# Attention into a gated unit on one Trainium2 core: gated loads, one causal select per chunk, and paired half-row transposes, with a new instruction order

## The chip, the cores and the metric

The kernel runs on one core of a Trainium2 chip. The metric is device time in microseconds (us). The engines go by the names that the profile gives them: PE is TensorE (PEld its weight loads), DVE is VectorE, ACT is ScalarE, POOL is GpSimd, and SP issues the DMA transfers. Each run has a state, fast or slow; only fast runs are compared, and it is said where that was not possible.

## The reference, cut to what matters

```python
# q, k, v: (8 batches, 8 heads, 576, 64); s: (8, 8, 576)
scores = q @ k.T / 8
cum    = cumsum(maximum(s, 0))
scores = where(causal, -1e9, scores + minimum(cum_k - cum_q, 0))
x      = softmax(scores) @ v                     # then heads side by side: (8, 576, 512)
gate_pre = sum(conv_w[k] * shift(x, 4 - k) for k in range(5))
out    = (sigmoid(gate_pre) * (x @ w_val)) @ w_out
```

## The kernel before

The work is cut into 32 chunks: eight batches times four pairs of heads. Each step of a chunk is a task with an engine, an assumed duration and a priority. A small planner in the kernel simulates the engines with those durations and fixes, while the program is built, the order in which each engine gets its instructions. The chip then follows that order; only the waits are decided at run time. Priorities (`DUE`) and choices of engine (`CHOICE`) are tables of constants, found by a search against the planner's own clock.

```python
def qk_T(b, p):                       # TensorE: one pair of heads, 8 full transposes, one PSUM bank
    pt = slot["qt", b, p] = bank(("qt", b, p), 128, 1024, BF16)...
    for which in range(2):
        for j in range(4):
            nc.tensor.transpose(pt[:, which, j * 128:(j + 1) * 128],
                                qkbs[which][b % 2][:, j, p * 128:(p + 1) * 128], ident)

def mask(n, hh):                      # POOL: zero the future in the diagonal blocks, one head
    d = slot["Pt", n][:, hh, 0:512].rearrange("k (g q) -> k g q", g=4)
    nc.gpsimd.affine_select(out=d, in_=d, pattern=[[0, 4], [1, 128]], compare_op=ALU.is_ge,
                            fill=0.0, base=0, channel_multiplier=-1)

def tap(e, n, sh):                    # one tap of the causal convolution, on DVE or on POOL
    ...
    if e == "POOL":                   # two instructions
        nc.gpsimd.tensor_tensor(tmp[:, o:S], xs[...], r.to_broadcast(...), ALU.mult)
        nc.gpsimd.tensor_tensor(gp[:, o:S], tmp[:, o:S], gp[:, o:S] if o else xs[:, 2:], ALU.add)
    elif o:                           # one instruction
        nc.vector.scalar_tensor_tensor(gp[:, o:S], slot["x", n][...], r, gp[:, o:S], ALU.mult, ALU.add)
    ...

plan = Plan(dict(P=3, gp=2, th=6, ot=3, qkf=3))     # buffers per kind; ot: output tiles
...
add("POOL", 0.6, n + due("mask") + 0.01 * hh, lambda n=n, hh=hh: mask(n, hh), [t])   # for hh in 0, 1
...
t = add(("DVE", "POOL"), (0.73, 2.25), n + due("tap") + sh * due("dtap"), ..., pick=("tap", 4 * n + sh - 1))
...
plan.total = plan.run()
with tc.manual_schedule():
    for t in plan.order:
        t["emit"]()
```

Four taps a chunk make 128 taps; before, 18 of them run on POOL and 110 on DVE. ACT takes the exponentials (96 of 128x1024) and the tanh of the gate, DVE normalises, and POOL also casts Q and K and scales V by the decay weights `w`, which come from `s`.

## Time and profile before

| | before |
|---|---|
| time, median of 3 runs | 211.16 us (209.36 to 211.21) |
| span of the profiled run | 209.3 us |
| busiest engines | DVE 178.0, PE 175.4, ACT 163.1, POOL 161.9 us |
| chain that ended last | DVE 27%, ACT 24%, PE 23%, no POOL |
| mean granted clock of TensorE | 0.965 |

A busy time is a sum over one engine; the chain is the sequence of work that set the end, followed backwards through the waits. Four engines are busy for 77 to 85% of the span, so none is a bound alone. The lines themselves are in the prediction below.

### The profile page before, as it was taken

How to read it: one execution, taken by the hardware profiler on the slowest of the kernel's cores; microseconds unless marked ns; L12 is line 12 of the kernel's file. 1: busy time of each engine (PE TensorE's matmuls, PEld its weight loads, DVE VectorE, ACT ScalarE, POOL GpSimd, SP SyncE). 2: the span in 40 equal slices, each digit the busy share in tenths (PEclk: the TensorE clock that was granted, in tenths of full speed). 3: DMA queues.
4: the chain of work that ended last, by engine and by line, in shares of the span. 5: the costliest groups of instructions: out<-in, count | busy, mean ns of one | idle time of the engine just before them, and what ended most of it. 6: DMA issues, size and time to landing. Idle time of an engine off the chain costs nothing.

```text
span 209.3 us, 6007 instructions
## 1 busy us (share of the span) xinstructions
PE 175.4 (84%) x2392; PEld 119.4 (57%) x2411; DVE 178.0 (85%) x311; ACT 163.1 (78%) x205; POOL 161.9 (77%) x179
## 2 busy tenths in 40 slices
PE   1697885999969998689899799989899999979950
PEld 0455763475736766367665567565576556645620
DVE  3847969999888998669999999999999998999810
ACT  3279497778999899987996998799987998553330
POOL 4276486499959998999589999967975899999300
PEclk9999797599999999999999999999999999999995
DMA  4999999997999699999999821951149220222551
GB/s 147 238 279 288 361 147 216 354 271 207 244 281 323 138 319 221 323 297 226 222 383 307 190 107 25 184 147 49 54 110 219 81 77 1 99 104 75 180 180 61
DMA packets 69230, 40.48 MB, mean 193 GB/s; under 512 B 47109, under 2 KB 63493, under 8 KB 69194
## 3 DMA queue, kind: packets, MB, share of 16 engines
q1 hardware_dynamic: 69194, 40.01, 72.7%
q8 instruction: 21, 0.34, 0.7%
q14 instruction: 15, 0.12, 0.2%
HBM read 30.57 MB, written 9.44 MB: 191 GB/s over the span
## 4 chain that ended last, share of the span: by engine, by line
DVE 27%; ACT 24%; PE 23%; DMA 8%; issue 8%; SPq 7%; ACTq 0%; DVEq 0%
ACT P L592 13%; DVE gp L647 9%; PE banks L660 8%; DMA qkf<-in_moe_w_val_dram 6%; PE banks L672 6%; DVE xn L623 4%; PE banks L613 4%; ACT QKT L561 4%; ACT th L653 4%; DVE glu L666 3%; DVE gp L649 3%; PE banks L566 3%; SPq L515 3%; SPq L534 2%; ACT ot L677 2%
## 5 line engine op out<-in xcount | busy, mean ns | idle before, releaser
L592 ACT ACTIVATE P<-banks 128x1024 bf16<-128x1024 f32 x96 | 94.8, 1039 | 11.8 <-PE banks L566 9.9
L647 DVE SCALAR_TENSOR_TENSOR gp<-banks,ratio,gp 128x574 f32<-128x574 bf16 (+2 forms) x85 | 67.5, 804 | 2.4 <-POOL gp L645 1.7
L598 POOL TENSOR_SCALAR_AFFINE_SELECT P<-P 128x512 bf16<-128x512 bf16 x64 | 39.6, 640 | 11.3 <-ACT P L592 11.1
L566 PE MATMUL banks<-QKT 64*128 64x128 bf16 (+4 forms) x576 | 38.9, 249 | 8.8 <-ACT P L592 5.6
L660 PE MATMUL banks<-xT,wv 128*128 128x288 bf16 x256 | 41.7, 294 | 2.1 <-DVE glu L666 0.9
L672 PE MATMUL banks<-wo,glu 128*128 128x512 bf16 x141 | 38.3, 379 | 2.5 <-ACT QKT L561 0.8
L528 POOL TENSOR_TENSOR Vp<-vst,w 128x650 bf16<-128x650 f32 x29 | 37.6, 1316 | 1.3 <-DMA vst<-in_v_dram 1.3
L613 PE MATMUL banks<-Vp,P 128*128 128x65 bf16 x960 | 37.3, 198 | 1.3 <-ACT P L592 1.2
L613 PEld LDWEIGHTS <-P 128*128 128x128 bf16 x960 | 35.3, 101 | 5.4 <-issue 2.1
L566 PEld LDWEIGHTS <-QKT 64*128 64x128 bf16 x576 | 20.1, 97 | 27.0 <-issue 20.6
L653 ACT ACTIVATE th<-gp,halfw 128x576 f32<-128x576 f32 x32 | 25.2, 793 | 7.1 <-DVE gp L647 3.6
L660 PEld LDWEIGHTS <-wv 128*128 128x128 bf16 x256 | 22.8, 99 | 13.9 <-issue 6.1
L666 DVE SCALAR_TENSOR_TENSOR glu<-th,banks 128x288 bf16<-128x288 f32 x64 | 28.0, 445 | 1.1 <-PE banks L660 1.0
L623 DVE TENSOR_TENSOR xn<-banks,recs 128x640 bf16<-128x640 f32 x32 | 26.2, 818 | 0.3
L561 ACT COPY QKT<-banks 128x1024 bf16<-128x1024 bf16 x25 | 25.3, 1049 | 1.2 <-PE banks L557 1.1
L677 ACT COPY ot<-banks 128x512 f32<-128x512 f32 (+1 forms) x26 | 15.2, 587 | 11.4 <-PE banks L672 6.9
L672 PEld LDWEIGHTS <-glu 128*128 128x128 bf16 x160 | 14.6, 97 | 15.5 <-issue 2.7
L649 DVE SCALAR_TENSOR_TENSOR gp<-xT,ratio,banks 128x576 f32<-128x576 bf16 x25 | 20.1, 809 | 1.6 <-ACT xT L635 0.9
L644 POOL TENSOR_TENSOR tmp<-xT,ratio 128x576 f32<-128x576 bf16 (+3 forms) x18 | 20.6, 1142 | 1.0 <-ACT xT L635 0.5
L645 POOL TENSOR_TENSOR gp<-tmp,gp 128x573 f32<-128x573 f32 (+2 forms) x11 | 15.7, 1428 | 3.1 <-DVE gp L647 2.3
L631 PE MATMUL banks<-ident,xn 128*128 128x128 bf16 x160 | 14.2, 220 | 2.9 <-DVE xn L623 1.2
L518 POOL CAST qb<-qkf 128x2048 bf16<-128x2048 f32 x7 | 13.2, 1890 | 2.2 <-DMA qkf<-in_q_dram 2.2
(63 smaller groups left out, 169.2 us busy)
## 6 DMA issues: line engine op xcount, KB each, us to landing
out_dram<-ot SPq DMA_DIRECT2D x32, 256.0 KB, 2.9
qkf<-in_q_dram SPq DMA_DIRECT2D x7, 1024.0 KB, 8.5
qkf<-in_k_dram SPq DMA_DIRECT2D x7, 1024.0 KB, 9.9
vst<-in_v_dram SPq DMA_DIRECT2D x28, 256.0 KB, 5.4
vst<-in_v_dram SPq DMA_DIRECT2D x15, 128.0 KB, 4.0
first<-in_q_dram SPq DMA_DIRECT2D x4, 256.0 KB, 3.4
first<-in_k_dram SPq DMA_DIRECT2D x4, 256.0 KB, 3.4
tail<-in_q_dram SPq DMA_DIRECT2D x8, 128.0 KB, 8.7
```

The lines of the kernel that those rows point to most:

```text
L528: eng.tensor_tensor(Vps[b % 2][:, :, h], vst[:, :, h], w[:, :, b * 8 + 2 * p:b * 8 + 2 * p + 2].unsqueeze(3).to_broadcast([128, NKB, 2, 65 ...
L561: copy[e](QKTs[b % 2][:, :, p, 0:512].rearrange("d w (x j) -> d w x j", j=4), slot["qt", b, p].rearrange("d w (j x) -> d w x j", j=4))
L566: nc.tensor.matmul(ps[:, hh, c0:c0 + nq], QKTs[b % 2][r, 1, p, k0:k0 + 128], QKTs[b % 2][r, 0, p, q0:q0 + nq], **kw)
L592: nc.scalar.activation(out=slot["Pt", n][:, :, step * 512:(step + 1) * 512], in_=slot["s", n, step], func=AF.Exp, scale=0.125)
L598: nc.gpsimd.affine_select(out=d, in_=d, pattern=[[0, 4], [1, 128]], compare_op=ALU.is_ge, fill=0.0, base=0, channel_multiplier=-1)
L613: nc.tensor.matmul(ps[:, hh, qb * 65:qb * 65 + 65], lhsT, Vps[b % 2][:, kb, 2 * p + hh, :], start=(kb == 0), stop=(kb == qb))
L623: nc.vector.tensor_tensor(xns[b % 2][:, :, p * 128:(p + 1) * 128].rearrange("t g (h d) -> t h g d", h=2), pv[:, :, :, 0:64], recs[:, n].un ...
L647: nc.vector.scalar_tensor_tensor(gp[:, o:S], slot["x", n][:, 0:S - o], r, gp[:, o:S], ALU.mult, ALU.add)
L653: nc.scalar.activation(out=th, in_=slot["g", n], func=AF.Tanh, scale=halfw[:, n % 4, :])
L660: nc.tensor.matmul(ps, wv[:, dc, c * 128:(c + 1) * 128], xTs[b % 2][:, dc, 2 + o:290 + o], start=(dc == 0), stop=(dc == 3))
L666: nc.vector.scalar_tensor_tensor(glus[b % 2][:, c, o], slot["t", n][:, o], 1.0, slot["v", n, hf], ALU.add, ALU.mult)
L672: nc.tensor.matmul(ps, glus[b % 2][:, c, WIN[i]:WIN[i] + 128], wo[:, c, :], start=(c == 0), stop=(c == 3))
```

## The change

Its intent: save TensorE time with half-row transposes that run two at a time, save POOL time with one select for both heads, and keep early loads from piling up in the DMA queue. Output buffers grow from three to five, and all priorities and engine choices are searched anew.

```diff
-DUE = dict(w=-69.33, lwv=-4.26, ...)          # (cut: 71 priorities before, 90 after, all new)
+DUE = dict(w=-211.74, lwv=14.18, ..., lq0d=12.42, ...)
+BEHIND = 11.22
-              tap="0000000010...0000",        # 18 taps on POOL
+              tap="0000010010...0000",        # 28 taps on POOL
 ...
                 if e == "SP":
-                    idle_at[e] = now + 0.06
                     dma_free = max(dma_free, now + 1.2) + us
+                    idle_at[e] = max(now + 0.06, dma_free - BEHIND)     # the planner's gate
 ...
-    plan = Plan(dict(P=3, gp=2, th=6, ot=3, qkf=3))
+    plan = Plan(dict(P=3, gp=2, th=6, ot=5, qkf=3))
 ...
+    def qk_T2(b, m):                 # two pairs of heads, 32 half-row transposes, two PSUM banks
+        for w in range(2):
+            for p in range(2):
+                for j in range(4):
+                    for g in range(2):
+                        r = slice(64 * g, 64 * g + 64)
+                        nc.tensor.transpose(pt[:, g, w, p, j, :],
+                            qkbs[w][b % 2][r, j, (2 * m + p) * 128:(2 * m + p + 1) * 128], ident[r, r])
 ...
-    def mask(n, hh):
-        d = slot["Pt", n][:, hh, 0:512].rearrange("k (g q) -> k g q", g=4)
-        nc.gpsimd.affine_select(out=d, in_=d, pattern=[[0, 4], [1, 128]], ...
+    def mask(n):
+        d = slot["Pt", n][:, :, 0:512].rearrange("k h (g q) -> k h g q", g=4)
+        nc.gpsimd.affine_select(out=d, in_=d, pattern=[[0, 2], [0, 4], [1, 128]], ...
 ...
-                es += [t] if i else [add("POOL", 0.6, ..., mask(n, hh), [t]) for hh in range(2)]
+                es += [t] if i else [add("POOL", 0.75, n + due("mask"), lambda n=n: mask(n), [t])]
```

The tasks of the first batch (loads, casts, scalings) also get searched priorities instead of fixed ones, so the start may come in another order too.

## The prediction

> **What bounds the kernel now.** I read the page first for the engines' busy time, then the table by stretches, then the chain of waits, then the groups by line, and last the timeline of single engines for the spacing of instructions. First, busy time:
>
> ```profile
> PE 175.4 (84%) x2392; PEld 119.4 (57%) x2411; DVE 178.0 (85%) x311; ACT 163.1 (78%) x205; POOL 161.9 (77%) x179
> ```
>
> Four engines lie within 16 us of each other; no single one is the bound by itself. The table by stretches (length, then busy time of PE, PEld, DVE, ACT, POOL) shows where the other 31 us of DVE, the longest, went:
>
> ```profile
> 0.00:30.00 30.00, 20.21 (x277) 15.44 (x278) 19.13 (x35) 18.85 (x26) 17.17 (x34) 0.94 0.95 246
> 30.00:190.00 160.00, 143.52 (x2056) 97.65 (x2071) 150.33 (x261) 138.57 (x173) 139.32 (x142) 0.98 0.74 191
> 190.00:209.30 19.30, 11.68 (x66) 6.31 (x65) 8.52 (x17) 5.64 (x9) 5.46 (x5) 0.89 0.40 135
> ```
>
> In the middle 160 us DVE is 94% busy (150.3), PE 90%, ACT and POOL 87%. DVE idles about 11 us in the start, 10 in the middle and 11 in the end. So the middle is bound by DVE with PE and ACT close behind, and start and end are bound by latency. The chain that ended last agrees:
>
> ```profile
> DVE 27%; ACT 24%; PE 23%; DMA 8%; issue 8%; SPq 7%; ACTq 0%; DVEq 0%
> ```
>
> It passes through three engines in turn; GpSimd (POOL) is not on it at all, so POOL had slack before. Its end is a plain wait for a buffer: the last ACT copy of an output tile waits until a store has left one of the three output buffers.
>
> ```profile
> 199.24 0.59 ACT ot L677
> ...
> 199.84 3.50 DMA out_dram<-ot
> ...
> 203.44 0.59 ACT ot L677
> ```
>
> The timeline has the last output matmuls from 197.31 for 4.48 us, that is to 201.8, so this wait costs about 203.4 - 201.8 = 1.6 us.
>
> **What the Trainium skill says.** "TensorE: Matmul & The Clock Gate", Part 3 (Packing small matmuls): matmuls in different row groups run at the same time in one array, their starts a few ns apart. The trace agrees. Seven score matmuls of 64 columns, alternating between the halves, take 0.27 us, the last alone about 0.20: (0.27 - 0.20)/6 = 12 ns apart. Four full transposes of 128 columns take 0.39, one 0.22: (0.39 - 0.22)/3 = 57 ns apart.
>
> ```profile
> 60.62 0.27 PE L566 MATMUL banks<-QKT 64*128 64x64 bf16 x7 [0.51 <-ACT QKT L561]
> 72.38 0.39 PE L557 MATMUL banks<-ident,qb 128*128 128x128 bf16 x4
> ```
>
> "TensorEngine Tiling (Array Packing)", Key Properties: changing the tiling mode drains TensorE. The trace fits: weight loads of the score matmuls sit idle 20.6 us in 55 places with no other releaser than "issue". "GPSIMD Engine Reference", 3.1: a one-input body costs about one cycle per element, two inputs some 2.6. The trace agrees in the first: a select over 128 elements took 0.304 us when undisturbed, over 512 0.634 us (median), so 0.86 ns an element.
>
> **The change part by part.** The order in which the built program stands on each engine gives counts; durations are from the groups by line:
>
> ```profile
> L598 POOL TENSOR_SCALAR_AFFINE_SELECT P<-P 128x512 bf16<-128x512 bf16 x64 | 39.6, 640 | 11.3 <-ACT P L592 11.1
> L647 DVE SCALAR_TENSOR_TENSOR gp<-banks,ratio,gp 128x574 f32<-128x574 bf16 (+2 forms) x85 | 67.5, 804 | 2.4 <-POOL gp L645 1.7
> L644 POOL TENSOR_TENSOR tmp<-xT,ratio 128x576 f32<-128x576 bf16 (+3 forms) x18 | 20.6, 1142 | 1.0 <-ACT xT L635 0.5
> L561 ACT COPY QKT<-banks 128x1024 bf16<-128x1024 bf16 x25 | 25.3, 1049 | 1.2 <-PE banks L557 1.1
> ```
>
> Transposes. In seven of eight batches, two pairs of heads took 16 transposes, 16 x 57 ns = 0.91 us; now 32 half-row ones at 12 to 15 ns, 0.38 to 0.48 us. Fourteen groups save 14 x 0.45 = 6.3 us of PE. They also share the tiling of the score matmuls. I counted the changes between half-row and full matmuls in both orders: 126 before, 124 after, so no drains are saved. PE goes from 175.4 to about 169. What it costs: a group takes two PSUM banks through two evacuations, and a pair's scores wait for both.
>
> Select. 64 of 512 elements become 32 of 1024. Start to start, two old ones take 1.20 us. One new one should take 0.63 + 512 x 0.86 ns = 1.07 us, some 1.04 start to start. Saving 32 x 0.16 = 5 us of POOL. (The kernel's own plan charges 0.75 us for it; I see nothing in the trace that supports so little.)
>
> The new order moves work as well. Gate taps on POOL, each a multiply and an add, go from 18 to 28. Start to start in the timeline one takes 2.46 to 2.72 us, so 10 x 2.55 = +25.5 us on POOL. On DVE taps fall from 110 to 100, -8.0 us; but 14 instead of 7 evacuations of Q and K (+7 x 1.217 = +8.5), 6 instead of 3 of tails (+1.3), 12 instead of 14 output copies (-1.4), 19 instead of 26 x copies (-3.2) and two more casts (+0.8) leave DVE at 178.0 - 2.0 = 176.0. ACT: -7 x 1.049 - 3 x 0.594 + 7 x 0.664 + 2 x 0.587 - 0.6 = -3.9, to 159.2. POOL: 161.9 - 5 - 0.6 + 25.5 = 181.8. So POOL, off the chain before, becomes the longest engine.
>
> Output buffers. Five instead of three: the 1.6 us wait in the end should go.
>
> Gated transfers. The gate is only in the plan that makes the order; the chip has no new wait. Its effect is that loads stand later and stores earlier in one queue. Waits for DMA outside the start are small (the longest sum, 2.2 us, for the cast of Q), so I give this about 1 us. In the start, the tails of Q and K and the conv weights are now issued before the first head pair: the first Q issue moves from 2.0 us to about 2.7 us, but the second pair's follows at once. About zero.
>
> **The sum.** DVE's view: 209.3 - 2.0 (its own work) - 1.6 (end) - 1 (loads), and PE's 6.3 us count in proportion to its 23% of the chain, 1.5 us: about 203 us. POOL's view: its cast of the second batch's K, which lay at 25.8 us, can come at about 24.7. From there on it has 13 large casts x 1.84, 7 tail casts x 0.56, 28 selects x 1.04, 7 small selects x 0.61, 28 scalings of V x 1.235 and 28 taps x 2.58: 23.9 + 3.9 + 29.1 + 4.3 + 34.6 + 72.2 = 168 us, ending at 192.7 without idling. Before, POOL's last tap ended at 195.8 and the run at 209.3, 13.5 us later; less 1.6, 12. That gives 204.7 plus POOL's idle time, of which I take 4 us (it was about 21 in 160, but an engine that lags finds its input ready): 208.7. Between 203 and 208.7, as neither is a full bound, the profiled span should be about 205; timed runs lie some 1 us above (211.16 to the profile's 209.3 span, though one run had 209.36): 206.0 us.
>
> **The rivals.** First, POOL becomes a real bound: the chain then runs through taps and selects on POOL, tanh waits for POOL, and the time is 209 to 214. For it: the count of 28 taps, of which the last three on one chunk stand in a row near the end. Against: its slack of 21 us in the middle. Second, the select is much cheaper than linear, as the plan believes: 32 x 0.3 = 9 us less on POOL, whose view becomes about 199, DVE's binds, and with a better order the time is 200 to 203. Against: the slope of 0.86 ns an element. Third, half-row transposes do not overlap, each as slow as 57 ns or the pair serialised: PE gains nothing or loses (32 x 57 ns = 1.8 us a group, +13 us), and the time is 212 or more. Against: score matmuls with the same shape are 12 ns apart. Fourth, all savings lie off the chain: 209 to 211. For it: three engines share the chain and two of them barely lose work.
>
> **Range and chances.** 2% faster means below 206.9. The two views straddle that, and the rivals give 200 to 203 and 209 to 214. The order was searched anew with more freedom, which usually takes some idle out of the middle and speaks for faster. I take 206.0, 200.5 to 212, with 0.52 faster, 0.38 the same, 0.10 slower.
>
> **What would show it.** In the changed profile: half-row transposes with a spacing of 12 to 15 ns and PE near 169; a select of about 1.07 us; POOL near 181 and the busiest, now with a share of the chain; DVE near 176; no wait of an output copy for a store in the last 15 us. The prediction is wrong on the low side if the select is below 0.85 us or DVE idles less than 5 us in its middle; on the high side if tanh waits for POOL in many places, or if score matmuls wait for the paired evacuations.

## The result

The changed kernel takes **222.21 us** (median of 4 runs, 221.21 to 222.49) against 211.19 us (209.36 to 212.93, 4 runs) for the kernel before, timed in the same rounds: a ratio of 1.0544, with a 95% interval from 1.0467 to 1.0621. It is 11 us slower, and lies above the predicted range. Ratios here are the mean time of one kernel's runs over that of the other's of the same rounds, so they are not quite the ratio of the medians quoted. Executions over 1.5% slower than the fastest of the same kernel are left out of the means.

The busy times of the changed kernel:

```profile
PE 176.0 (80%) x2616; PEld 116.6 (53%) x2635; DVE 179.4 (81%) x304; ACT 160.0 (72%) x203; POOL 184.4 (84%) x166
```

POOL went from 161.9 to 184.4 and is the busiest. PE did not fall. The busiest engine before was DVE with 178.0 us in 209.3, so 31.3 us of the span lay beside its work; now they are 220.8 - 184.4 = 36.4. The changed kernel by stretches (columns as in the prediction: window, length, then busy time and number of instructions of PE, PEld, DVE, ACT, POOL, then granted clock, DMA share, GB/s):

```profile
0.00:30.00 30.00, 17.19 (x221) 12.40 (x221) 19.02 (x34) 15.55 (x21) 17.05 (x28) 1.00 0.94 243
30.00:190.00 160.00, 135.82 (x2198) 91.15 (x2215) 140.25 (x235) 129.37 (x161) 150.75 (x126) 0.94 0.70 186
190.00:220.80 30.80, 22.99 (x201) 13.04 (x200) 20.10 (x36) 15.10 (x23) 16.62 (x14) 0.96 0.31 110
```

In the middle 160 us, POOL rose from 139.3 to 150.8, and every other engine did *less* than before: DVE 140.3 instead of 150.3, PE 135.8 instead of 143.5, ACT 129.4 instead of 138.6. That work is left over for the end: after 190 us POOL has 16.6 us to do instead of 5.5, DVE 20.1 instead of 8.5. The chain of the changed kernel, by engine and by line, names what they waited for:

```profile
POOL 49%; DVE 17%; issue 13%; PE 10%; ACT 4%; DMA 3%; SPq 2%; POOLq 0%; ACTq 0%; DVEq 0%
POOL P L619 11%; POOL Vp L534 10%; POOL tmp L665 10%; POOL gp L666 9%; DVE gp L668 5%; PE banks L634 3%; POOL qb L524 3%; PE banks L693 3%; POOL kb L524 3%; DMA sp<-in_s_dram 3%; DVE gp L670 3%; POOL P L624 2%; DVE glu L687 2%; DVE xn L644 1%; ACT P L613 1%
```

An engine that was on no link of the chain now carries half of it, through selects (L619), scalings of V (L534) and taps (L665 and L666). The view of waits (who waited, for what: us in all, times, longest) shows how it holds the others:

```profile
PEld L634 <- POOL P L619: 6.7, 9, 1.5
ACT th L674 <- POOL gp L666: 6.6, 6, 1.8
PE banks L634 <- POOL P L619: 4.3, 6, 1.2
```

The attention product on PE (L634) now waits for a select, 4.3 us in matmuls and 6.7 in weight loads (the two overlap); before, its matmuls idled 1.3 us in all, and not for POOL. ACT's tanh waits 6.6 us for taps on POOL, 3.3 before.

The groups by line of the changed kernel that answer to those in the prediction (engine, operation, tiles, count | busy us, mean ns | idle before it, what ended most of that):

```profile
L668 DVE SCALAR_TENSOR_TENSOR gp<-banks,ratio,gp 128x573 f32<-128x573 bf16 (+2 forms) x72 | 58.1, 809 | 4.8 <-POOL gp L666 3.8
...
L619 POOL TENSOR_SCALAR_AFFINE_SELECT P<-P 128x1024 bf16<-128x1024 bf16 x32 | 35.2, 1101 | 8.8 <-ACT P L613 8.8
...
L665 POOL TENSOR_TENSOR tmp<-xT,ratio 128x574 f32<-128x574 bf16 (+3 forms) x28 | 32.0, 1143 | 0.5
...
L582 ACT COPY QKT<-banks 128x1024 bf16<-128x1024 bf16 x17 | 16.8, 1023 | 0.0
```

The select of 1024 columns takes 1.10 us, as the prediction had it and not the 0.75 of the plan. The 28 multiplies take 32.0 us; with the adds (35.7 and 4.8 us by shape) the taps fill 72.5 us of POOL, 2.59 us each.

The timeline of PE in the changed kernel, near the first paired transposes and at a later place (start, duration of the group, instructions):

```profile
31.17 0.61 PE L578 MATMUL banks<-ident,qb 64*128 64x64 bf16 x16
...
115.03 0.41 PE L578 MATMUL banks<-ident,qb 64*128 64x64 bf16 x16
```

One such transpose takes 0.19 us at full clock (median of the operation), so 16 are (0.41 - 0.19)/15 = 15 ns apart: the halves do overlap. At 31 us the granted clock was low (0.66 from 30 to 50 us) and the whole is slower.

In the start, the chain of the changed kernel runs through the load of `s`:

```profile
4.88 5.87 DMA sp<-in_s_dram
...
15.50 0.45 ACT w L481
16.08 3.37 POOL Vp L534
```

Before, this load was the first to be issued, at 0.81 us, and the decay weights `w` came at 8.13 us. Now seven loads go first, `w` comes at 15.50, and POOL's first scaling of V takes 3.37 us at 16.08, where an instruction of the same kind took 1.28 us at 12.02 in the kernel before. The first reciprocal, that is the first chunk through attention, comes at 21.5 us instead of 17.3. In the same stretch of the timeline DVE does two scalings of V itself:

```profile
16.74 1.56 DVE L534 TENSOR_TENSOR Vp<-vst,w 128x650 bf16<-128x650 f32 x2
18.23 1.50 DVE L524 CAST qb<-first 128x512 bf16<-128x512 f32 x1
```

The Trainium skill ("GPSIMD Engine Reference", 1. Specifications) says that GpSimd's interfaces to the on-chip memory are shared with VectorE and that the two contend when a VectorE instruction has two inputs there or runs in a two-port mode. The trace fits: POOL's 3.37 us and DVE's cast of 1.50 us (0.41 for the next one like it) lie side by side. No run here isolates it, and which engine is held up differs: in the run e2_s_first below, POOL's first scaling starts just before DVE's two and takes 1.28 us, while DVE's two take 2.62 us instead of 1.56:

```profile
14.45 2.62 DVE L534 TENSOR_TENSOR Vp<-vst,w 128x650 bf16<-128x650 f32 x2
```

In the end, the wait for an output buffer is gone. The timeline of ACT in the changed kernel:

```profile
207.36 1.44 ACT L674 ACTIVATE th<-gp,halfw 128x576 f32<-128x576 f32 x2 [1.78 <-POOL gp L666]
...
214.76 0.59 ACT L698 COPY ot<-banks 128x512 f32<-128x512 f32 x1 [1.14 <-PE banks L693]
```

The last copy waits for PE, not for a store. But the last tanh waits for a POOL tap that ends at 207.3 us; before, POOL's last tap ended at 195.8. From 200 us on the chain itself runs through DVE and PE and not through POOL.

### The profile page after: what moved, and what is told of

Same layout as the page of the kernel before. It is cut to its first block, busy times and chain, and to the rows that moved or that the text cites. A ratio compares the mean times of both kernels' runs of the same rounds, so it can differ in the third digit from the quotient of the medians.

```text
span 220.8 us, 6459 instructions
## 1 busy us (share of the span) xinstructions
PE 176.0 (80%) x2616; PEld 116.6 (53%) x2635; DVE 179.4 (81%) x304; ACT 160.0 (72%) x203; POOL 184.4 (84%) x166
## 4 chain that ended last, share of the span: by engine, by line
POOL 49%; DVE 17%; issue 13%; PE 10%; ACT 4%; DMA 3%; SPq 2%; POOLq 0%; ACTq 0%; DVEq 0%
POOL P L619 11%; POOL Vp L534 10%; POOL tmp L665 10%; POOL gp L666 9%; DVE gp L668 5%; PE banks L634 3%; POOL qb L524 3%; PE banks L693 3%; POOL kb L524 3%; DMA sp<-in_s_dram 3%; DVE gp L670 3%; POOL P L624 2%; DVE glu L687 2%; DVE xn L644 1%; ACT P L613 1%
## 5 line engine op out<-in xcount | busy, mean ns | idle before, releaser
L668 DVE SCALAR_TENSOR_TENSOR gp<-banks,ratio,gp 128x573 f32<-128x573 bf16 (+2 forms) x72 | 58.1, 809 | 4.8 <-POOL gp L666 3.8
L587 PE MATMUL banks<-QKT 64*128 64x128 bf16 (+4 forms) x576 | 41.7, 254 | 14.2 <-ACT P L613 6.4
L634 PE MATMUL banks<-Vp,P 128*128 128x65 bf16 x960 | 39.2, 201 | 7.3 <-POOL P L619 4.3
L634 PEld LDWEIGHTS <-P 128*128 128x128 bf16 x960 | 36.3, 103 | 13.6 <-POOL P L619 6.7
L681 PE MATMUL banks<-xT,wv 128*128 128x288 bf16 x256 | 40.3, 297 | 3.4 <-DVE glu L687 1.5
L619 POOL TENSOR_SCALAR_AFFINE_SELECT P<-P 128x1024 bf16<-128x1024 bf16 x32 | 35.2, 1101 | 8.8 <-ACT P L613 8.8
L534 POOL TENSOR_TENSOR Vp<-vst,w 128x650 bf16<-128x650 f32 x29 | 38.8, 1357 | 1.8 <-ACT w L481 1.8
L666 POOL TENSOR_TENSOR gp<-tmp,gp 128x574 f32<-128x574 f32 (+2 forms) x24 | 35.7, 1489 | 1.9
L587 PEld LDWEIGHTS <-QKT 64*128 64x128 bf16 x576 | 19.7, 99 | 33.2 <-issue 26.3
L665 POOL TENSOR_TENSOR tmp<-xT,ratio 128x574 f32<-128x574 bf16 (+3 forms) x28 | 32.0, 1143 | 0.5
L670 DVE SCALAR_TENSOR_TENSOR gp<-xT,ratio,banks 128x576 f32<-128x576 bf16 x28 | 22.5, 807 | 4.0 <-ACT xT L656 3.2
L698 ACT COPY ot<-banks 128x512 f32<-128x512 f32 (+1 forms) x28 | 16.6, 594 | 9.4 <-PE banks L693 9.3
L582 ACT COPY QKT<-banks 128x1024 bf16<-128x1024 bf16 x17 | 16.8, 1023 | 0.0
L582 DVE COPY QKT<-banks 128x1024 bf16<-128x1024 bf16 x11 | 13.4, 1217 | 0.8 <-PE banks L578 0.8
```

The lines of the kernel that those rows point to most:

```text
L534: eng.tensor_tensor(Vps[b % 2][:, :, h], vst[:, :, h], w[:, :, b * 8 + 2 * p:b * 8 + 2 * p + 2].unsqueeze(3).to_broadcast([128, NKB, 2, 65 ...
L582: copy[e](QKTs[b % 2][:, :, 2 * m:2 * m + 2, 256 * g:256 * g + 256].rearrange("d w p (x j) -> d w p x j", j=4), slot["qt2", b, m][:, g].re ...
L587: nc.tensor.matmul(ps[:, hh, c0:c0 + nq], QKTs[b % 2][r, 1, p, k0:k0 + 128], QKTs[b % 2][r, 0, p, q0:q0 + nq], **kw)
L619: nc.gpsimd.affine_select(out=d, in_=d, pattern=[[0, 2], [0, 4], [1, 128]], compare_op=ALU.is_ge, fill=0.0, base=0, channel_multiplier=-1)
L634: nc.tensor.matmul(ps[:, hh, qb * 65:qb * 65 + 65], lhsT, Vps[b % 2][:, kb, 2 * p + hh, :], start=(kb == 0), stop=(kb == qb))
L665: nc.gpsimd.tensor_tensor(tmp[:, o:S], xs[:, 2 - sh + o:2 - sh + S], r.to_broadcast([128, S - o]), ALU.mult)
```

## The experiments

Three theories stood first. Theory 1: the ten taps that the new order gave to POOL make it a real bound. Theory 2: the late start (the load of `s`) costs the time. Theory 3: the paired transposes, with their joint wait, hold up the scores. Further rivals are the wide select and the new order as such. Where an edit is made "in place", the planned order is kept to the letter and only what one task emits is changed, so that the edit is not mixed with a new order. All twelve kernels gave correct results. The changed kernel itself (222.21 us, ratio 1.0544) was not timed again in these rounds, so a difference to it in microseconds is between medians of different rounds; the median of before moved between 210.3 and 211.7 us over them. The ratios to before are within rounds.

### Ten of POOL's 28 taps on DVE, in the changed kernel (e1_taps18)

```diff
     plan.total = plan.run()
+    ts = [t for t in plan.order if t["pick"] and t["pick"][0] == "tap" and t["eng"] == "POOL"]
+    for i, t in enumerate(ts):
+        if (i + 1) * 10 // len(ts) > i * 10 // len(ts):      # ten of 28, evenly spread
+            t["emit"] = partial(t["emit"].func, "DVE")
```

> The changed kernel, same order everywhere, but ten of the 28 gate taps that GpSimd does are done by DVE at the same places. Theory 1 (GpSimd is overloaded and sets the time): GpSimd loses about 10 x 2.58 = 25 us of work, DVE gains 8; GpSimd's share of the chain falls well below 49% and the time falls by 6 to 10 us, to 212 to 216. Theory 2 (the late start, from the late load of s, costs the time): at most 2 us less. Theory 3 (half-row transposes or paired evacuations hold up the scores): unchanged within 1 us, or worse because DVE has more.

Measured: 218.57 us (217.79 to 219.0), ratio to before 1.0354 [1.0259, 1.0448]. That is 3.6 us less than the changed kernel, about half of what theory 1 expected. Its busy times and chain:

```profile
PE 174.7 (80%) x2616; PEld 116.3 (54%) x2635; DVE 182.6 (84%) x314; ACT 159.9 (74%) x203; POOL 159.7 (74%) x146
...
DVE 36%; PE 21%; POOL 12%; issue 10%; ACT 8%; DMA 7%; SPq 3%; DVEq 0%; POOLq 0%; ACTq 0%
```

POOL's share of the chain fell from 49 to 12%: with ten taps less it is hardly on the path. But DVE, which has the taps now, is as long as POOL was: 182.6 us of work in a span of 217. The experiment moves the load more than it takes it away, and it does not give back the 11 us.

### The load of s issued first, in the changed kernel (e2_s_first)

```diff
     plan.total = plan.run()
+    plan.order.remove(t_s)
+    plan.order.insert(0, t_s)
```

> The changed kernel, same order everywhere but for the load of s, which is issued first as in the kernel before. Theory 2: the decay weights come about 3 us earlier than 15.5 us, the first scaling of V no longer waits, and the whole run is 3 to 5 us shorter, about 218. Theory 1: GpSimd starts its row of work up to 3 us earlier, so part of it is kept, 1 to 3 us. Theory 3: no change.

Measured: 220.1 us (219.06 to 220.54), ratio 1.0432 [1.0332, 1.0532]: 2.1 us less. `w` comes 1.8 us earlier, at 13.69 us, which is still 5.6 us later than before: the first step on `s` on DVE stands behind other work until 7.98 us. The first scaling on POOL, in the timeline of this run, is short again:

```profile
14.26 1.28 POOL L534 TENSOR_TENSOR Vp<-vst,w 128x650 bf16<-128x650 f32 x1 [1.05 <-ACT w L481]
```

So the start, for which the prediction allowed "about zero", costs 2 us.

### Full transposes in the changed kernel (e3_full_T)

```diff
         for w in range(2):
-            for p in range(2):
+            for g in range(2):
                 for j in range(4):
-                    for g in range(2):
-                        r = slice(64 * g, 64 * g + 64)
-                        nc.tensor.transpose(pt[:, g, w, p, j, :], qkbs[w][b % 2][r, j, (2*m+p)*128:...], ident[r, r])
+                    nc.tensor.transpose(pt[:, g, w, j, :], qkbs[w][b % 2][:, j, (2*m+g)*128:...], ident)
 ...                                          # (cut: the two copies out of PSUM follow the new layout)
```

> The changed kernel, same order and same PSUM pairs, but each group is 16 full transposes instead of 32 half-row ones. My count says TensorE gets 14 x 0.45 = 6 us more work, in the shadow of GpSimd: theory 1 expects 0 to 2 us more. Theory 3 in the form that half-row transposes are bad in themselves expects 2 us or more less.

Measured: 221.28 us (220.37 to 222.91), ratio 1.048 [1.0382, 1.0578], with these busy times:

```profile
PE 181.2 (82%) x2393; PEld 123.5 (56%) x2411; DVE 179.1 (81%) x304; ACT 160.1 (72%) x203; POOL 184.7 (83%) x166
```

The half-row form saves 181.2 - 176.0 = 5.2 us of PE (expected 6.3), and none of it is in the time: this kernel is even 0.9 us below the changed one, within the scatter. In this order PE was not what the others waited for. The joint wait for both evacuations is kept here, so this run does not test it; the searched runs at the end do.

### Two selects in the changed kernel (e4_two_selects)

```diff
-        d = slot["Pt", n][:, :, 0:512].rearrange("k h (g q) -> k h g q", g=4)
-        nc.gpsimd.affine_select(out=d, in_=d, pattern=[[0, 2], [0, 4], [1, 128]], ...)
+        for hh in range(2):
+            d = slot["Pt", n][:, hh, 0:512].rearrange("k (g q) -> k g q", g=4)
+            nc.gpsimd.affine_select(out=d, in_=d, pattern=[[0, 4], [1, 128]], ...)
```

> The changed kernel, same order, with two selects of 512 in place of one of 1024. Start to start 1.20 us instead of 1.06, so 32 x 0.14 = 4.5 us more of GpSimd. Theory 1: 2 to 4.5 us more, as GpSimd carries half of the chain. Theories 2 and 3: below 1 us.

Measured: 223.16 us (222.1 to 223.52), ratio 1.0571 [1.0472, 1.0671]. POOL's busy time rose by 3.3 us to 187.7 and the time by 1.0, where theory 1 had expected 2 to 4.5. The wide select is a small gain and no cause of the loss. POOL's share of the chain in this profile is 25% and not 49, with more to do on POOL: the chain of one profile tells where to look, and its shares are no measure of what an engine costs.

### Ten more taps on POOL, in the kernel before (e5_before_28taps)

The mirror of the first experiment: in the old order, ten of DVE's 110 taps, every eleventh, are emitted on POOL in place.

> The kernel before, its own order, but ten of DVE's 110 gate taps (every eleventh) are done by GpSimd in place, so 28 in all as in the changed kernel. GpSimd goes to about 187 us, DVE to 170. Theory 1 (the load of the busiest engine, plus 31 to 36 us of start, end and waits, sets the time): 187 + 33 = 220, slower by 3 to 5%. Rival (the new order and start are what costs, the taps are not): within 1% of the kernel before.

Measured: 235.17 us median of 4 runs. Three of these, the profiled one among them, count as slow because they lie over 1.5% above the fourth, so there is no ratio; the one fast run took 231.37 us, 20 us more than the 211.08 of before beside it. The expectation was far too low. In an order made for a DVE tap of 0.8 us, a POOL tap of 2.6 stands where others wait at once. One such wait in the profile of this (slow) run:

```profile
DVE gp L647 <- POOL gp L645: 19.3, 8, 4.1
```

So ten taps, each time other ones, are worth 3.6 us in one order and some 20 in another. The number of taps on POOL is no measure by itself; their places count.

### One select per chunk in the kernel before (e6_before_select)

The edit of the fourth experiment the other way round, in the old order: nothing is emitted for the first head, and one select for both at the second.

> The kernel before, its own order, with one select for both heads in place of two (the later of the two places). GpSimd loses 32 x 0.14 = 4.5 us, which was not on the chain: theory 1 expects no change within 1 us, perhaps 0.5 us worse as the select ends later for the first head. Rival (the select is on the way from the exponentials to the second matmul, so its latency counts): 2 us better or more.

Measured: 211.32 us (209.89 to 214.26, the highest a slow run), ratio 1.0023 [0.9948, 1.0099]; POOL fell from 161.9 to 156.7 us. Five microseconds were saved off the path, and the time stood still.

### Five output buffers in the kernel before (e7_before_ot5)

```diff
-        ot = slot["ot", b, i] = work("ot", (b, i), [128, DM], FP32)
+        slot["nout"] = slot.get("nout", 0) + 1
+        ot = slot["ot", b, i] = one.tile([128, DM], FP32, name=f"ot{slot['nout'] % 5}")
```

> The kernel before, its own order, with five output buffers used in turn instead of the three of the plan. My step of the prediction: the wait of the last output copies for a store disappears and the end comes 1.6 us sooner. Rival (the store queue is what ends the kernel, and it takes the same time): no change within 0.5 us.

Measured: 208.85 us (207.15 to 209.88), ratio 0.99 [0.9821, 0.9979]. The end of its chain, where before a store of 3.50 us stood between two copies, is now:

```profile
198.79 2.34 PE banks L672 x10
...
201.15 0.58 ACT ot L678
```

The wait is gone, and the gain of 1% (0.2 to 1.8%) holds the predicted 1.6 us; of the two parts that were tried in the kernel before, this one is worth time by itself and the select is not.

### Measured POOL costs in the plan of the changed kernel (e8_true_costs)

```diff
-... add("POOL", 0.75, n + due("mask"), ...
+... add("POOL", 1.06, n + due("mask"), ...
-... add(("DVE", "POOL"), (0.73, 2.25), n + due("tap") ...
+... add(("DVE", "POOL"), (0.73, 2.58), n + due("tap") ...
```

> The changed kernel with two numbers of its plan put right, 1.06 us for a select and 2.58 us for a GpSimd tap in place of 0.75 and 2.25; all choices and priorities the same, so the loads stay and only the order moves. If the order made from wrong costs is what hurts (work placed too early behind a GpSimd that lags): 3 to 5 us less, 217 to 219. If the load is what hurts: within 2 us of 222.

Measured: 228.73 us (228.36 to 229.51), ratio 1.0842 [1.0746, 1.0938]. Every engine has the instructions of the changed kernel (POOL 184.5 us busy), and only the order differs; it is 6.5 us worse. POOL has 6% of the chain:

```profile
PE 34%; ACT 20%; DVE 19%; issue 7%; POOL 6%; DMA 6%; SPq 4%; ACTq 0%; POOLq 0%; DVEq 0%
```

Neither outcome came. These priorities, searched with the low costs, did not get better when two costs were corrected. One thing besides the order differs: the granted clock of TensorE was 0.909 to 0.918 in all four runs, against 0.936 to 0.956 in those of the changed kernel, and PE was busy for 180.2 us instead of 176.0. How much of the 6.5 us is the order and how much the clock stays open.

### Both edits that helped, together (e9_taps18_s_first)

The first two diffs in one kernel.

> The changed kernel with both of the edits that helped it: ten of its 28 POOL taps given to DVE in place, and the load of s issued first. Apart they took 3.6 and 2.1 us off 222.2. Theory A (two separate causes, the load of POOL in the middle and the late decay weights in the start): the gains add, 216 to 217 us. Rival B (both gains are the same slack of POOL, since the late first scaling of V also sat on POOL): no better than the larger one, 218 to 219 us. If the 18 taps of before in the new order do not come near 211, the rest of the loss lies in the order itself and in POOL's selects being waited for.

Measured: 217.18 us (216.5 to 218.25), ratio 1.0318 [1.0253, 1.0384], with before at 210.53. That is 5.0 us less than the changed kernel; apart, the edits gave 3.6 and 2.1. They add up, nearly. With before's number of POOL taps and `s` first, 6 us of the 11 are still there. The busy times show DVE with 5.2 us more to do than before, and 215.1 - 183.2 = 31.9 us of the span beside its work, almost the 31.3 of before:

```profile
PE 173.5 (81%) x2635; PEld 114.2 (53%) x2635; DVE 183.2 (85%) x314; ACT 159.9 (74%) x203; POOL 157.4 (73%) x146
```

### The changed structure with an order searched against measured costs (e11_new_searched)

The half-row transposes, the one select and the five buffers stay. The gate stays only by name: its bound, `BEHIND`, came out of the search as 307.9 us instead of 11.22, and in a plan of some 206 us it never holds a load back. The plan is charged measured durations on POOL, and priorities and choices of engine are searched anew. The result has 25 taps on POOL and issues the load of `s` first.

```diff
-DUE = dict(w=-211.74, ...)   STAY, BEHIND, CHOICE of the change
+DUE, STAY, BEHIND = 307.896, CHOICE    # (cut) from a new search on the planner's clock
-                    idle_at[e] = max(now + 0.06, dma_free - BEHIND)
+                    idle_at[e] = max(now + (0.55 if us < 1.4 or us > 1.5 else 1.1), dma_free - BEHIND)
-    select 0.75, tap on POOL 2.25 (DVE 0.73), cast 1.95, tail cast 0.7
+    select 1.06, tap on POOL 2.58 (DVE 0.75), cast 1.86, tail cast 0.58
```

> The changed kernel's structure (half-row transposes, one select, five output buffers, gated loads) with an order searched anew against measured POOL costs (select 1.06, tap 2.58, cast 1.86) and 0.55 us per issued load; it has 25 taps on POOL. Replaying fixed orders at these costs gave 205.9 for before (measured 211.2), 213.9 for after (222.2), and 206.1 for this one. Theory A (the order, searched against POOL costs that were too low, is what lost the time): about 212 to 214 us, 8 or more better than after. Rival B (the structure itself costs: pairs of banks and the joint wait of two pairs' scores): 218 or more. Against A: the first order re-planned at measured costs, without a new search, came out 6.5 us worse than after.

Measured: 213.45 us (213.06 to 214.5), ratio 1.0138 [1.0076, 1.0199]. This is 8.8 us less than the changed kernel, the size that theory A had. Its busy times, whole and by stretches:

```profile
PE 174.0 (82%) x2635; PEld 113.9 (54%) x2635; DVE 172.1 (81%) x299; ACT 165.5 (78%) x209; POOL 174.1 (82%) x162
...
0.00:30.00 30.00, 18.33 (x281) 13.42 (x281) 20.91 (x36) 18.25 (x24) 17.10 (x31) 0.90 0.91 244
30.00:190.00 160.00, 143.02 (x2294) 93.88 (x2289) 140.31 (x245) 141.54 (x177) 152.46 (x129) 0.96 0.73 193
190.00:213.00 23.00, 12.67 (x68) 6.57 (x65) 10.90 (x20) 5.68 (x9) 4.56 (x4) 0.83 0.29 103
```

POOL is as full in the middle (152.5 us of 160) as in the changed kernel. But PE and ACT, beside it, get 7 and 12 us more done there, and what POOL has left for the end falls from 16.6 to 4.6 us. POOL holds 24% of the chain instead of 49. So the half-row transposes, the paired evacuations and the select are not what costs 11 us. But the run does not single out the order either: the new choices also took 10.3 us of work off POOL and 7.3 off DVE (ACT got 5.5 more), so the busiest engine has 174.1 us to do and not 184.4. The span beside that work, 211.8 - 174.1 = 37.7 us, did not shrink (36.4 in the changed kernel). Nor is the gate tested alone. Loads that come too late would be its direct harm, and the profile has none: after 30 us the view of waits of the changed kernel lists no wait of an engine for a transfer (the view goes down to 0.2 us).

### The old transposes, searched in the same way (e12_old_T_searched)

Full transposes of one pair each, one select, five buffers, no gate in the plan, the same costs and search; 23 taps on POOL.

> The structure of before (full transposes, one pair each) with one select and five output buffers, its order searched in the same way and for the same time against the same costs; 23 taps on POOL; 205.2 us in the replay against 205.9 for before. If the replay carries to the chip: 209 to 211 us, near the 208.9 of before with five buffers. If taps on POOL are the trouble even when planned at their cost, it is slower than before: 213 to 218, since the ten moved taps in before's own order cost 24 us. Against the run with half-row transposes it shows what these are worth when both orders are searched alike: by the replay +0.9 us, that is nothing.

Measured: 213.1 us (211.34 to 213.61), ratio 1.0093 [1.002, 1.0166]. Beside the last run there is no difference that the intervals can tell: the paired half-row transposes neither gain nor cost when both orders come from the same kind of search (one search each). It missed the 209 to 211 that the planner's clock suggested: orders searched there are not better on the chip than the one of before.

### The two harmless parts in the kernel before (e13_before_both)

The edits of the sixth and seventh experiment in one kernel.

> Before in its own order, with the two parts of the change that cost nothing on their own: five output buffers (alone 208.85 us, ratio 0.990) and one select per chunk (alone 211.32, ratio 1.002). Theory A (the select's 4 to 5 us of POOL time lie off the chain in this order, the buffers' 1.6 us on it): no better than the buffers alone, 208 to 209.5 us, ratio 0.985 to 0.995. Rival B (with the end's wait gone, the freed POOL time counts too): 205 to 207, ratio under 0.98. Either way it should be the fastest of all kernels run here.

Measured: 209.8 us (207.63 to 211.14, one of six runs slow), ratio 0.9937 [0.9877, 0.9996]. As theory A had it, the select adds nothing to the buffers; that this would be the fastest kernel of all did not come true. The lowest time is still that of the kernel before with five output buffers, about 1% under it (208.85 us, ratio 0.99), though the intervals of the two overlap.

## Why the prediction was wrong

The time was predicted at 206.0 and measured at 222.2 us. By the steps of the prediction:

**Right in kind and nearly in size.** The select: 1.07 us expected, 1.10 measured. Taps on POOL: 2.58 each expected, 2.59 measured. POOL's busy time 181.8 against 184.4, ACT's 159.2 against 160.0. POOL became the longest engine and tanh waited for it, which was the first rival. The half-row transposes overlap, 15 ns apart (and the score matmuls 12), which is wider than the few ns of the page that the prediction names. No tiling drains were saved: idle weight loads of the score matmuls with no other releaser went from 20.6 to 26.3 us; that these are drains is not shown by any run. The wait for an output buffer went, and it is worth 1 to 2 us where nothing else hides it. The gate's step of about 1 us fits: after 30 us, waits of engines for loads went from 2.8 us to none.

**Off in size.** DVE: 176.0 expected, 179.4 measured. PE: 169 expected, 176.0 measured, although the transposes saved 5.2 of the 6.3 us; the mean granted clock fell from 0.965 to 0.948, and other groups of matmuls took longer (the attention product 39.2 us instead of 37.3). Neither was shown to matter for the time. The step from the profiled span to the time was 1.7 us in the profiled runs of both kernels and not "some 1 us".

In the prediction's own terms the span came out as 220.8 instead of 205 us. The first two steps below are the whole of that, 3.7 and 12 us; the third and the fourth ask what lies behind the second.

**The first step that failed: "Between 203 and 208.7, as neither is a full bound".** Each view is an estimate of the span if that engine sets it. Two such estimates can't be averaged: the time is at least the larger, and lies above it by what the engines wait for each other. The profile of before had the size of that, 31.3 us beside the busiest engine's work; in the changed kernel it is 36.4.

**The second: "POOL's idle time, of which I take 4 us".** Its view can be laid beside the profile. POOL's cast of the second batch's K began at 29.17 us instead of 24.7 (+4.5). From there to the end of POOL's last tap at 207.3 there are 178.2 us for 168.2 of work, where the prediction had counted 168: the work was right to the microsecond, but 10 us were idle instead of 4 (+6). From there to the end it took 13.5 us and not 12 (+1.5). Together that is 12 us, from 208.7 to 220.8. An engine that lags does not find its input ready all the time: of these 10 us, POOL's selects idled 8.8 waiting for exponentials from ACT (before, 11.1 us in the whole run), hardly less than when POOL had slack. That its own lateness came back to it through PE and ACT would explain this, and is not shown.

**The third: the start, "about zero".** The prediction saw the tails of Q and K and the conv weights move ahead of the first head pair, and not that the load of `s` fell from the first place to the eighth. The decay weights came 7.4 us later. Moving `s` back brings them forward by 1.8 us and takes 2.1 us off; the rest of their delay lies in the order of the other engines in the start and was not tested.

**The fourth: "The order was searched anew with more freedom, which usually takes some idle out of the middle and speaks for faster".** The middle became idler, but for POOL: DVE idled 19.8 us of the 160 instead of 9.7, PE 24.2 instead of 16.5, ACT 30.6 instead of 21.4. The prediction itself noted that the plan charges 0.75 us for a select that should take 1.07, but did not ask what an order made with that cost is worth.

Ten taps back on DVE and `s` first give 5.0 us together. What the other 6 us are stays open. Two causes are left, as the work of the busiest engine and the rest of the span show:

| kernel | busiest engine | span | beside its work |
|---|---|---|---|
| before | DVE 178.0 | 209.3 | 31.3 |
| changed | POOL 184.4 | 220.8 | 36.4 |
| measured costs, same loads (e8) | POOL 184.5 | 227.8 | 43.3 |
| 18 taps and `s` first (e9) | DVE 183.2 | 215.1 | 31.9 |
| searched anew (e11) | POOL 174.1 | 211.8 | 37.7 |

One is the choice of engines. The change put 6.4 us more on the busiest engine; the run with 18 taps lies above before by about what DVE has more to do; and the run that was searched anew gains its 8.8 us with 10.3 us less on the busiest engine and no fewer waits. The other is the order, which the gate in the plan helps to make. With equal loads another order took 6.5 us more, part of it perhaps by the clock. No run has the changed kernel's loads in a better order, so none parts the two.

That the low costs in the plan are why this order is poor is argued. For it: replaying the fixed orders on the planner's clock with measured POOL costs gives 205.9 us for before and 213.9 for after, 8 of the 11 us. Against it: the replay is some 5 us below the chip for before and 7 to 8 for the runs searched anew, so it can miss 2 to 3 us of such a difference; the plan of before charged the same 2.25 us for a tap; and correcting the costs without a new search made the kernel slower. The new search also changed several things at once (25 taps instead of 28, other choices, `s` first, no gate in effect, the cost of issuing a load), so which of them helps stays open.

## What to carry to other kernels

When several engines are over 75% busy, never average estimates of single engines. The busiest engine's work plus the waits beside it in the old profile is only a first estimate, and too low for every new order here: it gives 184.4 + 31.3 = 215.7 us of the measured span of 220.8, and in the fifth experiment a sum of this kind, 220 us, fell short by 11 us and more. Before believing in a new table of orders and choices, add up each engine's work under it and lay the plan's cost of each operation beside the trace; correcting such costs without a new search made the kernel slower here. Work moved to a slower engine costs by where it stands and not by its sum, so test it in place: ten taps cost 4 us in one order and 20 in another.

## What the Trainium skill lacked or had wrong

- "GPSIMD Engine Reference", 3.1 and 4.1: they do not name the affine select. It took 0.64 us for 128x512 and 1.10 us for 128x1024 (bf16, in place). The slope, about 0.9 ns for each further element of a partition, is in line with the 1.03 cycles per element that 3.1 gives for short bodies (an estimate of 0.86 ns at the 1.2 GHz of section 1); the remaining 0.2 us of each has no figure there.
- "GPSIMD Engine Reference", 4.1 (Engine selection) puts GpSimd at about half of VectorE's speed for operations with two inputs. That compares one operation with one; the convolution tap is one instruction of 0.81 us on VectorE and two, together 2.59 us, on GpSimd, so 3.2 times as long.
- "TensorEngine Tiling (Array Packing)", Key Properties, has no figure for transposes in two row halves, and the few ns that "TensorE: Matmul & The Clock Gate", Part 3, shows between starts are less than was seen here: 64x64 transposes came 15 ns apart where the clock was full, and 16 took 0.61 instead of 0.41 us where it was low.
- No page has a figure for the order of the first loads: issuing one small load first instead of eighth brought its consumer forward by 1.8 us and the end by 2.1.
